# Negative part times slope moved to ScalarE, one VectorE addition a pair of tiles, and three groups of VectorE products and sums moved to GpSimd, in a fused recurrence and feed-forward kernel

## The chip, the cores and the metric

The kernel runs on one core of a Trainium2 chip. The core has TensorE (PE: matrix products, with weight loads that the profile keeps apart as PEld), VectorE (DVE), ScalarE (ACT), GpSimd (POOL) and SyncE (SP, which here only issues transfers). Each engine works through its own list of instructions in order, and semaphores hold an instruction until what it needs is there. The metric is the device time of one execution in microseconds. Before the change the median of three runs is 622.16 us (620.33 to 623.74).

## The reference: what is computed

A gated linear recurrence runs for 4 batches and 8 heads over 768 positions with head size 48, and its output, as 3072 tokens of width 384, goes through a feed-forward block with 2048 hidden units and a leaky activation that has a slope of its own for every hidden unit.

```python
f = 1.0 / (1.0 + np.exp(-f_logit))
for t in range(S):
    state = f[:, :, t, :, None] * state + np.einsum('bhd,bhde->bhde', k[:, :, t], v[:, :, t])
    y[:, :, t] = np.einsum('bhd,bhde->bhe', q[:, :, t], state)
x = y.transpose(0, 2, 1, 3).reshape(B * S, H * D)
h = x @ w_in
g = np.maximum(h, 0.0) + alpha * np.minimum(h, 0.0)
out = g @ w_out
```

## The kernel before

Positions are cut into chunks of 128, and batches into pairs, so there are 6 x 2 = 12 steps (`steps`, L726). A step handles 256 tokens and passes through four stages, written as generators: `prepare` (key letter P: loads, sigmoid, products of decays, scaled copies of q and k), `carry` (S: scores between halves of a chunk, and the state), `attend` (O: scores inside 32 positions, the product with v and the state, the transposed result `xT`) and `network` (n: the feed-forward block). The order in which pieces of these generators are written is a string (`FIRST` and `USUAL`, L31 to L37). For TensorE, VectorE and ScalarE it is the order in their instruction lists (L734); GpSimd and SyncE get their lists from the framework's own scheduler. In the usual order a round holds the network of one step, the scores and state of the next, and the preparation of the one after that.

The parts that the change and the prediction touch, in the order of a usual round:

- `network`, first half. For each of 8 pairs of hidden tiles TensorE makes `ph` (L618), 128 hidden units by two tiles of 256 tokens, in one PSUM bank of a pool of four (`net`). ScalarE writes `neg`, the negative part with its sign turned (L623; `neg` has two buffers). VectorE then computes `neg * om + ph`, once for each tile of the pair (L625), into `gate`; `om` is one minus the slope.
- After the pairs 3 and 7, `sums` (L693) makes four sums or differences of gate tiles, 128 x 512 elements each, into `S` (L702). They feed a product of two-by-two blocks that needs seven block products in place of eight. In step 0 (`plain`) the product with `w_out` is done the ordinary way, without sums.
- `network`, second half (L655 to L689): block products `pa`, `pb`, `pc`, `pd`, `pa`, `pc`, `pe`, each of eight matmuls of 128 x 192, in banks of the same pool, and VectorE's combinations of them (L661). The eighth matmul of `pa` reads the last gate pair; `pc` reads the sums. The first `ph` of the next network takes over the bank of `pb`, so it waits until L661 has read it.
- `prepare`. ScalarE: sigmoid (L279), two copies (L280, L282), four strided copies (L314). VectorE: L287 to L294, two scans (L317, L319), L321, L347, then products L330 to L406, a 32 x 32 transpose (L401), and at the end the products of decays over a half chunk `f64` (L414), 48 x 8 elements each.
- `attend`: VectorE picks scores into `ad` (L526, L541), ScalarE copies them into `A` (L563, eight copies in a step, four for each batch `u` of the pair), TensorE multiplies `A` with v and the state (`py`, L574), ScalarE copies `py` to `y` (L583), and ten transfers on the queues of SP, ACT and POOL lay it out as `xT` for the next network (L603).
- `moved` (L488), called once in `carry` and once in `attend`: the state is multiplied by its decay `f64` (L494, 48 x 768 elements) and the new part is added (L498).
- GpSimd issues the loads of f, q, k and v (L266, L276) and two transfers of `xT` in each step; apart from set-up it computes nothing.

Of the kernel before, what the change touches and what calls it, by code (L numbers as in the profile page):

```python
# [14 lines left out]
AF = mybir.ActivationFunctionType  # L15
ALU = mybir.AluOpType
# [5 lines left out]
U = 2  # L22
# [36 lines left out]
def kernel(  # L59
# [30 lines left out]
    nc = tc.nc  # L90
    B, NC, _, HP, _ = qT.shape
    DM = v.shape[-1]
    H = 2 * HP
    D = DM // H
# [36 lines left out]
    NH, DH = NF // 2, DM // 2  # L131
# [122 lines left out]
    def halves(cc):  # L254

        return slice(CH * cc, CH * cc + CH), slice(CH * (1 - cc), CH * (1 - cc) + D)

    def prepare(bp, c, x):
# [152 lines left out]
        for cc in range(0 if c else 1, NC2 if c < NC - 1 else 1):  # L411
            for par in range(2):
                g64 = by64[rows(par), :, cc, :, NB]
                nc.vector.tensor_tensor(f64[halves(cc)[1], :, par:H:2].rearrange("p u h -> p (u h)"),  # L414
                                        g64[:, :, 0], g64[:, :, 1], ALU.mult)
        yield
        for cc in range(0 if c else 1, NC2):
# [14 lines left out]
    def carry(bp, c, x):  # L432
# [55 lines left out]
        def moved(cc):  # L488

            of, to = halves(cc)[1], halves(1 - cc)[1]  # L490
            was, then = (vs[bp][p, a, :, 0:DM].rearrange("p u (h e) -> p u h e", e=D)
                         for p, a in ((of, cc), (to, 1 - cc)))
            if c or cc:
                nc.vector.tensor_tensor(then, was, f64[of].unsqueeze(3).broadcast_to((D, U, H, D)), ALU.mult)  # L494
            for par in range(2):
                now = pd[rows(par), cc, 0:U * HP * D].rearrange("p (u h e) -> p u h e", u=U, e=D)
                if c or cc:
                    nc.vector.tensor_tensor(then[:, :, par:H:2], then[:, :, par:H:2], now, ALU.add)  # L498
                else:
                    nc.scalar.copy(then[:, :, par:H:2], now)  # L500
# [108 lines left out]
    def network(bp, c, x):  # L609
        i = f"{bp}_{c}"  # L610
        xT = x["T"]
        plain = (bp, c) == steps[0]
        for f in range(NH):
            ph = bank(f"ph{f}_{i}")
            tiles = (2 * f, 2 * f + 1) if plain else (f, f + NH)
            for kt in range(NK):
                for j, m in enumerate(tiles):
                    nc.tensor.matmul(ph[:, j * T:(j + 1) * T], lhsT=w_in_sb[:, kt, m * 128:(m + 1) * 128],  # L618
                                     rhs=xT[:, kt], start=(kt == 0 and j == 0), stop=(kt == NK - 1 and j == 1),
                                     skip_group_check=True)  # L620
            neg = work.tile([128, 2, T], F32, tag="neg", name=f"neg{f}_{i}")
            phv = ph.rearrange("p (j t) -> p j t", j=2)
            nc.scalar.activation(neg, phv, AF.Relu, scale=-1.0)  # L623
            for j, m in enumerate(tiles):
                nc.vector.scalar_tensor_tensor(gate[:, m % NH, m // NH], neg[:, j], om[:, m:m + 1], phv[:, j],  # L625
                                               ALU.mult, ALU.add)
            if not plain and f % 4 == 3:
                sums(slice(f - 3, f + 1))
            yield

        def store(u, o):
            t0 = ((U * bp + u) * NC + c) * C
            nc.sync.dma_start(out=out[t0:t0 + C], in_=o)

        if plain:
            po = [bank(f"po{u}_{i}") for u in range(U)]
            for n, (f, u) in enumerate([(f, u) for f in range(NF) for u in range(U)]):
                nc.tensor.matmul(po[u][:, 0:DM], lhsT=gate[:, f % NH, f // NH, u * C:(u + 1) * C], rhs=w_out_sb[:, f],  # L638
                                 start=(f == 0), stop=(f == NF - 1))
                if n % 8 == 7 and n != U * NF - 1:  # L640
                    yield
            for u in range(U):
                o = work.tile([128, DM], F32, tag="o", name=f"o{u}_{i}")
                nc.scalar.activation(o, po[u][:, 0:DM], AF.Copy, scale=UP)
                store(u, o)
            yield
            return

        a11, a12, a22 = (lambda f, j=j, u=u: gate[:, f, j, u * C:(u + 1) * C] for j, u in ((0, 0), (1, 0), (1, 1)))
        s1, s2, s3, s4 = (lambda f, n=n: late["S"][:, n, f] for n in range(4))  # L650
        b11, t1, b21, b22 = (lambda f, r=r, d=d: w_out_sb[:, NH * r + f, DH * d:DH * (d + 1)]
                             for r, d in ((0, 0), (0, 1), (1, 0), (1, 1)))
        t2, t3, t4 = (lambda f, t=t: late[t][:, f] for t in ("t2", "t3", "t4"))

        def product(to, of, by, more=False):  # L655
            for f in range(NH):
                nc.tensor.matmul(to[:, 0:DH], lhsT=of(f), rhs=by(f), start=(f == 0 and not more), stop=(f == NH - 1),  # L657
                                 skip_group_check=True)

        def plus(to, of, by, scale=UP):  # L660
            nc.vector.scalar_tensor_tensor(to, of[:, 0:DH], scale, by, ALU.mult, ALU.add)  # L661

        o0, o1 = (work.tile([128, DM], F32, tag="o", name=f"o{u}_{i}") for u in range(U))
        kept, u2, u3 = (late["C"][:, n] for n in range(3))
        pa, pb = (bank(f"p{n}_{i}") for n in "ab")
        product(pa, a11, b11)
        product(pb, a22, t4)
        nc.scalar.activation(kept, pa[:, 0:DH], AF.Copy, scale=UP)
        yield
        pc, pd = (bank(f"p{n}_{i}") for n in "cd")  # L670
        product(pc, s2, t2)
        product(pd, s1, t1)
        plus(u2, pc, kept)
        yield
        product(pa, a12, b21, more=True)
        product(pc, s3, t3, more=True)
        plus(o0[:, DH:DM], pd, u2)
        nc.scalar.activation(o0[:, 0:DH], pa[:, 0:DH], AF.Copy, scale=UP)  # L678
        yield
        pe = bank(f"pe_{i}")  # L680
        product(pe, s4, b22)
        plus(u3, pc, kept)
        plus(o1[:, 0:DH], pb, u3, -UP)
        plus(o1[:, DH:DM], pd, u3)
        store(1, o1)
        yield
        plus(o0[:, DH:DM], pe, o0[:, DH:DM])
        store(0, o0)
        yield  # L689
# [3 lines left out]
    def sums(fs_):  # L693

        s = late["S"]
        u0, u1 = slice(0, C), slice(C, T)
        of = lambda j, u: gate[:, fs_, j, u]
        for to, x_, y_, op in ((s[:, 0, fs_], of(0, u1), of(1, u1), ALU.add),
                               (s[:, 1, fs_], s[:, 0, fs_], of(0, u0), ALU.subtract),
                               (s[:, 2, fs_], of(0, u0), of(0, u1), ALU.subtract),  # L700
                               (s[:, 3, fs_], of(1, u0), s[:, 1, fs_], ALU.subtract)):
            nc.vector.tensor_tensor(to, x_, y_, op)  # L702

    def halves_of_w_out():

# [93 lines left out]
```

## Time and profile before

| | |
|---|---|
| median of three runs | 622.16 us (620.33 to 623.74) |
| the profiled execution: span from its first to its last instruction | 622.1 us |
| its time beside the span | no other time is given for this execution; the median of the runs is 0.06 us from its span |
| granted TensorE clock | 1.000 |
| PE busy | 592.1 us (95%) |
| PEld busy | 529.8 us (85%) |
| VectorE busy | 497.1 us (80%), 997 instructions |
| ScalarE busy | 246.6 us (40%), 466 instructions |
| GpSimd busy | 63.0 us (10%), 117 instructions |

The share of busy time is a mean over stages of different kinds. The first 43.7 us hold the first preparation and scores, with TensorE busy 20.8 us; step 0's network runs to 102.6 us; ten rounds of about 47.6 us follow, the last of them without a preparation; and from 579.9 us on there is only the last network. An idle time in brackets behind an instruction is that of its engine just before it, with what ended it. Idle time of an engine that bounds nothing costs nothing.

### The profile page before, as it was taken

Reading aid. Unit: us, or ns where it says so; the run is one execution under the profiler, and the core shown is the slowest. Engines: PE = TensorE matmul, PEld = TensorE weight load, DVE = VectorE, ACT = ScalarE, POOL = GpSimd, SP = SyncE. Lnnn points to the kernel's source line nnn. Section 1 sums busy time; section 2 is a strip of 40 time slices with the busy share of each in tenths; the row PEclk is TensorE's granted clock in tenths of the full one; section 3 lists DMA queues with packets and bytes.
Section 4 is the critical chain, followed back from the end, with each engine's and each line's share of the span. In section 5 each row is a group of like instructions: output and inputs, shape, how many; then the busy total and the mean of one; then the engine's idle time right before and its main releaser. Section 6 shows DMA issues by size and latency. Waiting matters only on the chain.

```text
span 622.1 us, 19062 instructions
## 1 busy us (share of the span) xinstructions
PE 592.1 (95%) x8212; PEld 529.8 (85%) x8212; DVE 497.1 (80%) x997; ACT 246.6 (40%) x466; POOL 63.0 (10%) x117
## 2 busy tenths in 40 slices
PE   3568999999999999999999999999999999999997
PEld 3457866898899899899899899899889889889997
DVE  7588998899898798798798798798888888762261
ACT  5677862441641272262261351352253243223110
POOL 9120010001000011001001001001001000000000
PEclk9999999999999999999999999999999999999999
DMA  9964632014404314214313313413313401201000
GB/s 290 367 234 155 190 85 52 36 36 108 98 8 96 72 35 107 67 35 95 79 35 90 84 35 88 86 36 86 87 36 85 87 3 26 53 2 27 26 0 26
DMA packets 68116, 50.43 MB, mean 81 GB/s; under 512 B 47168, under 2 KB 60608, under 8 KB 68032
## 3 DMA queue, kind: packets, MB, share of 16 engines
q1 hardware_dynamic: 56656, 25.01, 15.6%
q0 software_dynamic: 6864, 22.35, 12.7%
q10 hardware_dynamic: 4512, 1.85, 1.7%
q8 instruction: 65, 1.06, 0.7%
q14 instruction: 19, 0.16, 0.1%
HBM read 36.21 MB, written 4.72 MB: 66 GB/s over the span
## 4 chain that ended last, share of the span: by engine, by line
PE 88%; DVE 6%; ACT 3%; issue 2%; DMA 1%; ACTq 0%; DVEq 0%
PE ph L618 39%; PE pc L657 9%; PE pa L657 8%; PE pd L657 5%; PE pe L657 4%; PE pb L657 4%; PE py L574 4%; PE po L638 3%; PE raw L520 3%; PE qu L535 3%; PE pd L484 3%; PE off L444 1%; PE xt L592 1%; DVE gate L625 1%; DMA f<-in_fT 1%
## 5 line engine op out<-in xcount | busy, mean ns | idle before, releaser
L618 PE MATMUL ph<-xT,w_in_sb 128*128 128x256 f32 x1152 | 258.7, 382 | 0.7 <-DVE Csum L661 0.7
L618 PEld LDWEIGHTS ph<-xT,w_in_sb 128*128 128x128 f32 x1152 | 216.4, 190 | 33.4 <-issue 2.3
L623 ACT ACTIVATE neg<-ph 128x512 f32<-128x512 f32 x96 | 57.4, 598 | 200.8 <-PE ph L618 139.5
L625 DVE SCALAR_TENSOR_TENSOR gate<-neg,om,ph 128x256 f32<-128x256 f32 x192 | 82.7, 478 | 50.6 <-ACT neg L623 50.4
L657 PE MATMUL pc<-t,S 128*128 128x192 f32 x352 | 61.7, 329 | 0.0
L657 PE MATMUL pa<-w_out_sb,gate 128*128 128x192 f32 x352 | 61.3, 327 | 0.1
L657 PEld LDWEIGHTS pa<-w_out_sb,gate 128*128 128x128 f32 x352 | 57.9, 190 | 1.0 <-DVE gate L625 0.4
L657 PEld LDWEIGHTS pc<-t,S 128*128 128x128 f32 x352 | 57.3, 190 | 0.6
L526 DVE COPY_PREDICATED ad<-mraw,raw 128x256 f32<-128x256 int32 (+1 forms) x96 | 42.4, 442 | 11.1 <-PE raw L520 8.6
L541 DVE COPY_PREDICATED ad<-mquad,qu 128x224 f32<-128x224 int32 (+6 forms) x140 | 42.0, 300 | 6.2
L419 ACT COPY A<-q 48x512 f32<-48x512 f32 x44 | 27.2, 619 | 36.1 <-DVE q L368 35.7
L563 ACT COPY A<-ad 32x256 f32<-32x256 f32 x96 | 38.7, 403 | 1.4
L330 DVE TENSOR_TENSOR us<-us,fs 128x768 f32<-128x768 f32 (+5 forms) x60 | 36.8, 614 | 0.0
L678 ACT ACTIVATE o<-pa 128x192 f32<-128x192 f32 x11 | 3.7, 332 | 75.2 <-PE pa L657 72.3
L661 DVE SCALAR_TENSOR_TENSOR Csum<-pc,Csum 128x192 f32<-128x192 f32 x22 | 7.9, 357 | 30.3 <-PE pc L657 30.1
L287 DVE TENSOR_TENSOR qd<-qd,f 128x768 f32<-128x768 f32 (+2 forms) x36 | 27.2, 756 | 6.0 <-ACT qd L282 6.0
L520 PEld LDWEIGHTS raw<-qd,k 48*32 48x32 f32 x1536 | 18.5, 109 | 15.3 <-issue 13.1
L520 PE MATMUL raw<-qd,k 48*32 48x80 f32 x1536 | 24.0, 243 | 7.6 <-issue 4.4
L702 DVE TENSOR_TENSOR S<-gate 128x512 f32<-128x512 f32 x44 | 30.3, 688 | 0.8
L657 PE MATMUL pe<-w_out_sb,S 128*128 128x192 f32 x176 | 30.4, 326 | 0.0
L657 PE MATMUL pd<-w_out_sb,S 128*128 128x192 f32 x176 | 30.4, 326 | 0.0
L657 PE MATMUL pb<-t,gate 128*128 128x192 f32 x176 | 30.4, 326 | 0.0
(101 smaller groups left out, 758.3 us busy)
## 6 DMA issues: line engine op xcount, KB each, us to landing
w_out_raw<-in_w_out SPq DMA_DIRECT2D x8, 767.8 KB, 5.8
w_in_raw<-in_w_in SPq DMA_DIRECT2D x8, 767.2 KB, 11.9
q<-in_qT POOLq DMA_DIRECT2D x11, 512.0 KB, 4.2
f<-in_fT POOLq DMA_DIRECT2D x11, 512.0 KB, 4.5
k<-in_kT POOLq DMA_DIRECT2D x11, 512.0 KB, 4.9
out<-o SPq DMA_DIRECT2D x24, 192.0 KB, 2.7
vs<-in_v POOLq DMA_DIRECT2D x22, 192.0 KB, 4.6
ksn<-kt SPq DMA_DIRECT2D x80, 32.0 KB, 2.0
```

The lines of the kernel that those rows point to most:

```text
L287: nc.vector.tensor_tensor(qdv[d], qdv[d - 1][:, :, :, 1:5 - d], f[:, :, 1:5 - d].rearrange("p (g i) r -> p g i r", i=NB), ALU.mult)
L330: nc.vector.tensor_tensor(us[:, :, UO[m]:UO[m] + 4 * n].rearrange("p g (i r) -> p g i r", r=4), us[:, :, skip:skip + 4 * n].rearrange("p g ...
L419: nc.scalar.copy(A[halves(cc)[1], :, par * HP:(par + 1) * HP, CH * cc:CH * (cc + 1)], q3[rows(par)].rearrange("p (u h c) s t -> p u h c (s ...
L520: nc.tensor.matmul(raw[DB * j:DB * (j + 1), par, hp * C:hp * C + QW], lhsT=k[r_, g * DB:(g + 1) * DB], rhs=qd[r_, g], start=True, stop=True)
L526: nc.vector.copy_predicated(adu[:, :, :, d:4], mraw[:, d, :, d:4].bitcast(I32).unsqueeze(1).broadcast_to((128, H, NB, n)), rv[:, :, QO[d]: ...
L541: nc.vector.copy_predicated(ad[:, u, :, :, 4 * m:DB], mquad[:, lo:lo + n].bitcast(I32).unsqueeze(1).unsqueeze(1).broadcast_to((128, 2, HP, ...
L563: nc.scalar.copy(A[s_, u, :, s_], ad[s_, u].rearrange("p r h t -> p (r h) t"))
L618: nc.tensor.matmul(ph[:, j * T:(j + 1) * T], lhsT=w_in_sb[:, kt, m * 128:(m + 1) * 128], rhs=xT[:, kt], start=(kt == 0 and j == 0), stop=( ...
L623: nc.scalar.activation(neg, phv, AF.Relu, scale=-1.0)
L625: nc.vector.scalar_tensor_tensor(gate[:, m % NH, m // NH], neg[:, j], om[:, m:m + 1], phv[:, j], ALU.mult, ALU.add)
L657: nc.tensor.matmul(to[:, 0:DH], lhsT=of(f), rhs=by(f), start=(f == 0 and not more), stop=(f == NH - 1), skip_group_check=True)
L702: nc.vector.tensor_tensor(to, x_, y_, op)
```

## The change

Four edits:

1. The product of the negative part and `om` is done by ScalarE, in place in `neg`, one instruction for each tile of a pair (192 in all). VectorE's `neg * om + ph` becomes a plain addition of `neg` and `ph`: for step 0 still one for each tile, for the other eleven steps one over both tiles of a pair, 128 x 512 elements.
2. The four sums of `sums` go from VectorE to GpSimd (88 instructions).
3. The product of state and decay in `moved` goes from VectorE to GpSimd (20 instructions).
4. The products of decays `f64` go from VectorE to GpSimd (40 instructions).

The lists of instructions change accordingly. On ScalarE the two multiplications stand right behind the `neg` that they work on, ahead of what followed it. On GpSimd the four second sums of a round are split: three, then the four decay products of the next step, then the fourth sum, then the state product for the next step, the load of f, the state product of this step, and only then the load of v and the two transfers of `xT`. On TensorE the order of the matmuls is unchanged.

```diff
@@ prepare
-                nc.vector.tensor_tensor(f64[halves(cc)[1], :, par:H:2].rearrange("p u h -> p (u h)"),
+                nc.gpsimd.tensor_tensor(f64[halves(cc)[1], :, par:H:2].rearrange("p u h -> p (u h)"),
                                         g64[:, :, 0], g64[:, :, 1], ALU.mult)
@@ carry, moved(cc)
             if c or cc:
-                nc.vector.tensor_tensor(then, was, f64[of].unsqueeze(3).broadcast_to((D, U, H, D)), ALU.mult)
+                nc.gpsimd.tensor_tensor(then, was, f64[of].unsqueeze(3).broadcast_to((D, U, H, D)), ALU.mult)
@@ network
             nc.scalar.activation(neg, phv, AF.Relu, scale=-1.0)
             for j, m in enumerate(tiles):
-                nc.vector.scalar_tensor_tensor(gate[:, m % NH, m // NH], neg[:, j], om[:, m:m + 1], phv[:, j],
-                                               ALU.mult, ALU.add)
+                nc.scalar.activation(neg[:, j], neg[:, j], AF.Copy, scale=om[:, m:m + 1])
+            if plain:
+                for j, m in enumerate(tiles):
+                    nc.vector.tensor_tensor(gate[:, m % NH, m // NH], neg[:, j], phv[:, j], ALU.add)
+            else:
+                nc.vector.tensor_tensor(gate[:, f], neg, phv, ALU.add)
             if not plain and f % 4 == 3:
                 sums(slice(f - 3, f + 1))
@@ sums
-            nc.vector.tensor_tensor(to, x_, y_, op)
+            nc.gpsimd.tensor_tensor(to, x_, y_, op)
```

## The prediction, made blind

> **What bounds the kernel now.** First the page: busy shares and the chain that ended last.
>
> ```profile
> span 622.1 us, 19062 instructions
> PE 592.1 (95%) x8212; PEld 529.8 (85%) x8212; DVE 497.1 (80%) x997; ACT 246.6 (40%) x466; POOL 63.0 (10%) x117
> ...
> PE 88%; DVE 6%; ACT 3%; issue 2%; DMA 1%; ACTq 0%; DVEq 0%
> ```
>
> TensorE carries 88% of the chain. VectorE's 80% is a mean, so the stages come next (stretch, its length, then busy time of PE, PEld, DVE, ACT, POOL).
>
> ```profile
> 102.60:152.00 49.40, 48.89 (x785) 43.80 (x783) 44.32 (x87) 18.47 (x36) 4.47 (x7) 1.00 0.24 63
> 389.00:436.60 47.60, 47.53 (x664) 43.26 (x669) 41.42 (x86) 17.87 (x36) 4.47 (x7) 1.00 0.29 68
> ```
>
> A usual round leaves TensorE idle for 0.07 us of 47.6. Less work on VectorE can win nothing in such a round; what is late in it costs its full lateness. So I looked in the timeline of that round for places without slack.
>
> ```profile
> 389.89 0.36 DVE L661 SCALAR_TENSOR_TENSOR o<-pb,Csum 128x192 f32<-128x192 f32 x1
> ...
> 390.60 5.05 PEld L618 LDWEIGHTS ph<-xT,w_in_sb 128*128 128x128 f32 x24 [0.17 <-DVE o L661]
> ...
> 416.18 0.60 ACT L623 ACTIVATE neg<-ph 128x512 f32<-128x512 f32 x1 [2.04 <-PE ph L618]
> 416.68 2.17 ACT L314 COPY us<-qd 128x256 f32<-128x256 f32 x4
> 416.81 0.87 DVE L625 SCALAR_TENSOR_TENSOR gate<-neg,om,ph 128x256 f32<-128x256 f32 x2 [0.33 <-ACT neg L623]
> ...
> 418.96 3.33 ACT L563 COPY A<-ad 32x256 f32<-32x256 f32 x8
> 421.23 2.16 PE L574 MATMUL py<-A,vs 128*64 128x64 f32 x64
> ...
> 426.29 0.36 DVE L661 SCALAR_TENSOR_TENSOR Csum<-pc,Csum 128x192 f32<-128x192 f32 x1 [1.51 <-PE pc L657]
> ```
>
> There are two. ScalarE runs from the last `neg` (416.18) to the last `A` copy (422.29) without a pause, and the second half of `py` wants that copy at 421.23 + 1.04 = 422.27: slack nil. VectorE's list ends at 390.25, and the next `ph` waited 0.17 us for it: slack nil again.
>
> Last, how GpSimd's reads of SBUF stand beside VectorE's two-input instructions, which only the start shows.
>
> ```profile
> 6.49 1.00 POOL L166 COPY mquad<-inq 128x28 f32<-128x28 f32 x7
> 7.44 3.24 POOL L174 COPY mhalf<-inq 128x12 f32<-128x12 f32 x6
> 7.49 0.96 DVE L287 TENSOR_TENSOR qd<-qd,f 128x768 f32<-128x768 f32 x1 [1.01 <-ACT qd L282]
> ...
> 11.91 1.19 DVE L321 TENSOR_TENSOR us<-us,f 128x1024 f32<-128x1024 f32 x1
> 12.16 2.19 POOL L190 COPY dense<-ident 128x48 f32<-128x48 f32 x2
> 13.03 1.24 DVE L347 TENSOR_TENSOR k<-k,kr 128x1024 f32<-128x1024 f32 x1
> ```
>
> Seven small copies take 1.00 us while VectorE is idle; six smaller ones take 3.24 us beside its products, and the last two 2.19 us, ending at 14.35 where L347 ends (14.27). Each copy waits for a VectorE instruction to end: the two exclude each other. These copies are too short to show whether a long GpSimd read holds VectorE in turn.
>
> **The sum** is made against the execution's span of 622.1 us; the median of the runs, 622.16, is the same within 0.01%, so nothing is added for what lies around the span.
>
> *Negative part times slope on ScalarE.* 192 instructions of 128 x 256 out of SBUF, scaled from a column. Nearest rows: L563's copy of 256 elements at 403 ns (constant scale), L623's at 598 ns for 512. I take 0.42 us each, 0.85 us a pair; ends 0.70 (overlapping as L314's do) and 1.0. On paper 192 x 0.42 = 81 us, in 375 us of idle ScalarE; in most rounds it lies in the 2 us gaps ahead of `neg`. It does not in the run from the last `neg`. There: `neg` of pair 4, then L279 to L282, move 0.85 us; VectorE's L287, which waits for L282, and the pair-5 addition behind it end at 416.4 in place of 415.7; the last `neg` needs that buffer, so it starts at 416.4 (+0.2); its two multiplications add 0.85; L314, L668 and L563 follow, about 1.1 us late (0.9 to 1.2), and with no slack at `py` so is TensorE. Inside this lies the last gate pair: ready at 418.6 (was 417.25 for its first tile), where the eighth matmul of `pa` wants its weights at 418.1; 0.5 us of the 1.1. Against it stands the 0.17 us wait of `ph`. Seven rounds (199 to 532 us) have this order: 7 x (1.1 - 0.17) = **+6.5 us**.
>
> *The addition.* 128 x 512 with one input in PSUM: L498 takes 552 ns at 384 elements, L702 688 at 512; I take 0.69 (0.65 to 0.75) for two L625 starts of 0.43. That saves 0.17 us a pair, off the path except as counted above.
>
> *What leaves VectorE.* Behind the last gate pair of a usual round: four sums 2.54 us (417.72 to 420.26), one L494 0.99, four L414 0.72, and the 1.51 us in which it waits for `pc`. From 417.68 to 437.85 (390.25 a round later) it now needs 20.17 us; 14.4 remain. They begin at 418.6.
>
> *What GpSimd must do meanwhile.* Four second sums, four L414, two L494; VectorE's L498 waits for the second L494. No GpSimd addition is in this trace. Lower end: a one-input copy (178 ns at 4 elements, 198 at 28: 0.83 ns an element), 0.60 us at 512. Upper end: the select of 128 elements at 742 ns scaled by four, 2.97 us, although that one itself sat beside L317. The copy is the nearest kind; with two inputs I count its elements twice: 0.17 + 512 x 1.66 = 1.02 us for a sum, 1.45 for L494, 0.18 for L414. Together 4.1 + 2.9 + 0.7 = 7.7 us. Since neither runs beside the other's reads, they add up: 418.6 + 14.4 + 7.7 = 440.7, where `ph` could go at 438.0 + 1.1 = 439.15. Stall 1.55 us, 7 x 1.55 = **+10.9**. At 0.60 us a sum (0.81 for L494, 4.7 us in all) there is none; at 2.97 (4.45 for L494) 21.5 us and a stall of 15.3 us a round.
>
> The Trainium skill, SBUF — State Buffer, section "Who interferes with whom", states that a VectorE instruction with two SBUF inputs contends with a GpSimd instruction that reads SBUF, whole instruction against whole instruction, the later one fully blocked. The trace agrees for GpSimd as the later one (3.24 us for six tiny copies); VectorE as the later one no run here shows. By that rule this term stands; without it the term is nothing.
>
> *The other rounds.* Round 1 (102.6 to 152.3): the first sums now fall among L721 and L287, the last gate pair is ready at about 132.75 (was 131.78); VectorE's 20.9 us to its last L661 (152.68) lose 5.2; 132.75 + 15.7 + 7.7 = 156.15: **+3.5**. Round 2: gates at 179.5, 14.35 us left, 201.55 against 200.1 for the next `ph`: 1.45, and 0.3 at `pa`: **+1.75**. The last two networks have no preparation behind them: 0.4 and 0.3 at `pa` and `py`: **+0.7**. Step 0 and the start: ScalarE's `y` copies (87.0) slip by some 5 us, covered up to 102.6; GpSimd's two L414 hold the second step's loads (14.4) about 1 us, covered since f is wanted at 33.06. Cost nil.
>
> *Queues passed.* On POOL the load of v and two `xT` transfers stand behind the second L494: issued at about 433 where it was 424.8, landing 4 us later at 437, wanted at 439. That cover is thin: it is what is late next, if GpSimd is slower than I take it. SP's sixteen `ksn` transfers need L401, which moves with VectorE and TensorE alike. Loads of f, k and q have over 20 us. The sums reach `pc` in time: third one ready at about 424.1, wanted at 425.6.
>
> Sum: 622.1 + 6.5 + 10.9 + 3.5 + 1.75 + 0.7 = **645**.
>
> **Rivals.** *One: GpSimd and VectorE run side by side.* Then VectorE ends at 433 at the latest plus its wait for `pc`, about 437.4, and stalls nobody; round 1 wins back its waits of 0.74 and 1.0 us. 622.1 + 6.5 - 1.7 + 0.3 + 0.7 = 628. For it: no VectorE row in the start is longer than its mean (L287 959 ns there and over all). Against it: the six copies.
>
> *Two: a GpSimd addition costs twice VectorE's rows*, 1.38 and 1.9 us: 10.0 us a round, stall 3.85. 7 x (0.93 + 3.85) + 5.8 + 4.05 + 0.7 = 44, so 666. For it: two inputs plus overheads that small copies hide; against it: memsets on both engines run alike (0.88 ns an element). The Trainium skill, GPSIMD Engine Reference, section 3.1, has 4497 against 2293 ns for 2048 elements, a ratio of 1.96; as an estimate by that page the sum is about 664. No run here shows it.
>
> *Three, the other side: not slower.* ScalarE's lateness doesn't reach `py`, and VectorE's relief takes away the waits of `ph` (8 x 0.17) and of round 1 (1.7): 619. Place: the last `A` copy against the second half of `py`. It decides when the two multiplications cost below 0.1 us in sum, as if they ran inside `neg`'s tail. For it: ScalarE idles 2.04 us just ahead of that `neg`. Against it: the idle lies before, not behind. That the edits don't reach the engines can be left out: the lists of instructions show them moved.
>
> **How the numbers follow.** 0.5% (3.1 us, near the spread of the runs) is about what can be told from no change. Chances: forecast 0.43 (sums between 0.6 and 1.25 us: 630 to 660), rival one 0.24, rival two 0.22, rival three 0.06, dearer still 0.05. Eight in ten: from 626, the lower side of rival one, to 668, just above rival two. Faster takes half of rival three, 0.03; the same the other half and the low end of rival one, 0.08; slower 0.89.
>
> **What would show it.** Right: VectorE idle or long products where GpSimd's sums run; `ph` waiting for L661 by 1 to 4 us in rounds 3 to 9; second half of `py` waiting for L563; TensorE idle 20 us more in all; VectorE about 60 us less busy unless blocked time counts as busy. Wrong: GpSimd sums near 0.7 us with VectorE rows unchanged (rival one), sums of 1.4 us (two), `py` not waiting (three), or `ph` waiting for the `xT` transfers from POOL.

## The result, and the profile after

The changed kernel takes 640.16 us (median of four runs, 638.81 to 642.40) where the kernel before, run beside it, takes 621.86 (620.33 to 623.74). The ratio is 1.0298, with a 95% interval of 1.0265 to 1.0330: 18.3 us slower. The prediction said 645, slower, with a range of 626 to 668.

The profiled execution of the changed kernel took 638.81 us, of which its span is 637.0, so 1.8 us lie around the span. Against the span before (622.1) that is 14.9 us more, less than the 18.3 between the medians, for two reasons: this execution is the lowest of its four, and the 622.1 us is one of the longer executions of the kernel before, whose spans in the runs timed here go from 618.3 to 623.1 with a median of 619.7. The places below are compared by the spans.

First the page of the changed kernel: span, busy shares, and shares of the chain that ended last.

```profile
span 637.0 us, 19255 instructions
...
PE 596.5 (94%) x8212; PEld 528.4 (83%) x8212; DVE 457.1 (72%) x761; ACT 329.1 (52%) x658; POOL 256.1 (40%) x265
...
PE 49%; DVE 23%; ACT 18%; issue 6%; SPq 1%; DMA 1%; ACTq 0%; DVEq 0%
```

VectorE is 40 us less busy, ScalarE 82 more and GpSimd 193 more. The chain, 88% TensorE before, now runs through VectorE and ScalarE for 41% of its length.

A usual round in windows, from the first `ph` of one network to that of the next (stretch, length, then busy time of PE, PEld, DVE, ACT, POOL):

```profile
401.38:450.60 49.22, 48.06 (x656) 43.28 (x656) 38.37 (x64) 24.72 (x52) 22.20 (x21) 1.00 0.27 66
```

The same stretch took 47.71 us before, with 0.07 us of it idle on TensorE; now TensorE is idle for 1.16. The view of waits says where over the whole run (engine, line, what it waited for: us, times, longest):

```profile
PE pa L661 <- DVE gate L630: 4.7, 9, 1.2
...
PE py L574 <- ACT A L563: 2.4, 8, 0.3
PE ph L618 <- DVE Csum L665: 2.4, 6, 0.4
...
PE po L642 <- DVE w_out_sb L234: 1.6, 1, 1.6
```

And the timeline of that round (start, length, engine, line; in brackets the idle time before it and what ended it):

```profile
427.23 0.60 ACT L623 ACTIVATE neg<-ph 128x512 f32<-128x512 f32 x1 [1.06 <-DVE gate L630]
427.86 0.91 ACT L625 ACTIVATE neg<-neg,om 128x256 f32<-128x256 f32 x2
428.68 2.15 ACT L314 COPY us<-qd 128x256 f32<-128x256 f32 x4
...
429.54 0.59 PE L661 MATMUL pa<-w_out_sb,gate 128*128 128x192 f32 x2 [0.36 <-DVE gate L630]
429.58 3.33 POOL L706 TENSOR_TENSOR S<-gate 128x512 f32<-128x512 f32 x2 [5.24 <-DVE gate L630]
...
430.07 1.77 DVE L319 TENSOR_TENSOR_SCAN ss<-fs,ones 128x289 f32<-128x289 f32 x1
...
431.77 2.22 DVE L321 TENSOR_TENSOR us<-us,f 128x1024 f32<-128x1024 f32 x1
...
432.87 2.26 POOL L706 TENSOR_TENSOR S<-S,gate 128x512 f32<-128x512 f32 x1
433.91 2.29 DVE L347 TENSOR_TENSOR k<-k,kr 128x1024 f32<-128x1024 f32 x1
...
434.27 1.03 PE L574 MATMUL py<-A,vs 128*64 128x64 f32 x28 [0.33 <-ACT A L563]
...
450.20 0.35 DVE L665 SCALAR_TENSOR_TENSOR Csum<-pc,Csum 128x192 f32<-128x192 f32 x1
...
450.58 0.36 DVE L665 SCALAR_TENSOR_TENSOR o<-pb,Csum 128x192 f32<-128x192 f32 x1
...
450.60 5.45 PE L618 MATMUL ph<-xT,w_in_sb 128*128 128x256 f32 x24 [0.40 <-DVE Csum L665]
```

The two multiplications stand between the last `neg` and L314, so the last gate pair and the last `A` copy are late for TensorE (0.36 and 0.33 us of idle). Behind the gate pair GpSimd and VectorE take turns: L319, L321 and L347, whose own lengths before were 0.74, 1.20 and 1.22 us, each last 1.02 to 1.07 us longer, while a GpSimd sum that takes 1.25 us on idle ground takes up to 2.26. At the end `ph` waits 0.40 us for VectorE. The three waits make 1.09 of the 1.51 us; the other 0.42 shows as busy time (48.06 against 47.64), in the matmuls beside the waits: from the first `pa` to the first `pb` it is 3.22 us where it was 2.60, and from the first `py` to the first `pc` 2.56 where it was 2.08. These 0.62 and 0.48, with the 0.40 at `ph`, are the whole loss of the round.

### The profile page after: what moved, and what is told of

Read it like the earlier page. It is cut to its first block, busy times and chain, and to the rows that moved or that the text cites. A ratio compares the mean times of both kernels' runs of the same rounds, so it can differ in the third digit from the quotient of the medians.

```text
span 637.0 us, 19255 instructions
## 1 busy us (share of the span) xinstructions
PE 596.5 (94%) x8212; PEld 528.4 (83%) x8212; DVE 457.1 (72%) x761; ACT 329.1 (52%) x658; POOL 256.1 (40%) x265
## 4 chain that ended last, share of the span: by engine, by line
PE 49%; DVE 23%; ACT 18%; issue 6%; SPq 1%; DMA 1%; ACTq 0%; DVEq 0%
PE ph L618 26%; PE pc L661 6%; DVE us L330 6%; ACT A L563 4%; ACT us L314 3%; ACT neg L625 3%; DVE qd L287 3%; ACT neg L623 2%; PE raw L520 2%; PE pd L484 2%; PE pe L661 2%; PE pa L661 2%; PE qu L535 2%; ACT qd L282 2%; PE pd L661 2%
## 5 line engine op out<-in xcount | busy, mean ns | idle before, releaser
L706 POOL TENSOR_TENSOR S<-gate 128x512 f32<-128x512 f32 x44 | 63.3, 1457 | 171.4 <-DVE gate L630 171.4
L630 DVE TENSOR_TENSOR gate<-neg,ph 128x512 f32<-128x512 f32 x88 | 59.6, 686 | 93.4 <-ACT neg L625 93.3
L625 ACT ACTIVATE neg<-neg,om 128x256 f32<-128x256 f32 x192 | 87.1, 500 | 3.2
L661 PE MATMUL pa<-w_out_sb,gate 128*128 128x192 f32 x352 | 64.5, 330 | 5.0 <-DVE gate L630 4.7
L266 POOL DMA_DIRECT2D k<-in_kT x11 | 8.0, 730 | 145.0 <-PE raw L520 145.0
L661 PEld LDWEIGHTS pa<-w_out_sb,gate 128*128 128x128 f32 x352 | 57.6, 190 | 9.4 <-DVE gate L630 8.8
L661 PE MATMUL pc<-t,S 128*128 128x192 f32 x352 | 62.1, 329 | 0.6 <-DVE Csum L665 0.3
L661 PEld LDWEIGHTS pc<-t,S 128*128 128x128 f32 x352 | 57.2, 190 | 1.8 <-DVE Csum L665 0.6
L330 DVE TENSOR_TENSOR us<-us,fs 128x768 f32<-128x768 f32 (+5 forms) x60 | 55.7, 928 | 0.0
L563 ACT COPY A<-ad 32x256 f32<-32x256 f32 x96 | 38.4, 400 | 1.4
L494 POOL TENSOR_TENSOR vs<-vs,f 48x768 f32<-48x768 f32 x20 | 37.6, 1882 | 1.3
L706 POOL TENSOR_TENSOR S<-S,gate 128x512 f32<-128x512 f32 x22 | 36.6, 1665 | 0.0
L414 POOL TENSOR_TENSOR f<-ps 48x8 f32<-48x8 f32 x40 | 27.3, 684 | 21.0 <-DVE ps L317 18.6
L574 PEld LDWEIGHTS py<-A,vs 128*64 128x64 f32 x768 | 25.7, 145 | 7.3 <-ACT A L563 5.1
```

Source lines behind the costliest of these rows:

```text
L330: nc.vector.tensor_tensor(us[:, :, UO[m]:UO[m] + 4 * n].rearrange("p g (i r) -> p g i r", r=4), us[:, :, skip:skip + 4 * n].rearrange("p g ...
L494: nc.gpsimd.tensor_tensor(then, was, f64[of].unsqueeze(3).broadcast_to((D, U, H, D)), ALU.mult)
L563: nc.scalar.copy(A[s_, u, :, s_], ad[s_, u].rearrange("p r h t -> p (r h) t"))
L625: nc.scalar.activation(neg[:, j], neg[:, j], AF.Copy, scale=om[:, m:m + 1])
L630: nc.vector.tensor_tensor(gate[:, f], neg, phv, ALU.add)
L706: nc.gpsimd.tensor_tensor(to, x_, y_, op)
```

## The experiments

Ten kernels were run, each timed beside the kernel before (medians of 621.41 to 622.21 us). Each table row gives the ratio to it, and then, from the profiled execution, the start of round 2, and the lengths of round 2, of rounds 3 to 9 (mean of seven) and of what follows (from the first `ph` of round 10 to the end). They are worked out from the starts of `ph` in the chain of work.

| kernel | time, us | ratio (95% interval) | start of round 2 | round 2 | rounds 3 to 9 | rest |
|---|---|---|---|---|---|---|
| before | 621.86 | 1 | 152.3 | 47.6 | 47.69 | 88.3 |
| changed | 640.16 | 1.0298 (1.0265 to 1.0330) | 156.6 | 48.2 | 49.05 | 88.9 |
| GpSimd's three edits | 629.98 | 1.0136 (1.0106 to 1.0166) | 152.8 | 49.1 | 48.28 | 88.4 |
| the gate's edit | 632.50 | 1.0180 (1.0142 to 1.0218) | 153.7 | 47.9 | 48.82 | 88.8 |
| only the decay products | 620.52 | 0.9984 (0.9966 to 1.0003) | 151.9 | 47.5 | 47.67 | 88.2 |
| memsets for the sums | 631.78 | 1.0169 (1.0139 to 1.0198) | 151.8 | 47.5 | 48.64 | 88.8 |
| only the sums | 627.23 | 1.0087 (1.0068 to 1.0106) | 156.0 | 47.4 | 47.59 | 88.7 |
| changed, last pair old | 636.51 | 1.0229 (1.0202 to 1.0255) | 154.9 | 49.1 | 48.49 | 88.1 |
| last pair and step 0 old | 632.92 | 1.0181 (1.0156 to 1.0206) | 153.3 | 49.0 | 48.45 | 88.0 |
| light: gate's edit with both old, decay products | 621.77 | 1.0006 (0.9990 to 1.0021) | 149.5 | 47.5 | 47.84 | 88.2 |
| changed, state product on VectorE | 635.96 | 1.0227 (1.0199 to 1.0254) | 156.5 | 48.2 | 48.65 | 88.8 |
| changed, state product twice | 686.72 | 1.1023 (1.0989 to 1.1056) | 166.2 | 53.9 | 53.71 | 88.8 |

One execution of each kernel is profiled. Two of the kernels take the same time as the kernel before: their rounds 3 to 9 agree with its within 0.15 us, but their round 2 starts 0.4 and 2.8 us earlier. So the start of round 2 is the least sure of these columns.

### The two halves of the change, each alone

GpSimd's three edits without the gate's:

```diff
-                nc.vector.tensor_tensor(f64[halves(cc)[1], :, par:H:2].rearrange("p u h -> p (u h)"),
+                nc.gpsimd.tensor_tensor(f64[halves(cc)[1], :, par:H:2].rearrange("p u h -> p (u h)"),
...
-                nc.vector.tensor_tensor(then, was, f64[of].unsqueeze(3).broadcast_to((D, U, H, D)), ALU.mult)
+                nc.gpsimd.tensor_tensor(then, was, f64[of].unsqueeze(3).broadcast_to((D, U, H, D)), ALU.mult)
...
-            nc.vector.tensor_tensor(to, x_, y_, op)
+            nc.gpsimd.tensor_tensor(to, x_, y_, op)
```

> The three groups of work go to GpSimd as in the change, but the gate stays as before (one scalar_tensor_tensor of VectorE for each tile, no multiplication on ScalarE). Theory A (two separate costs: ScalarE's multiplications make the second half of py late by 1.1 us a round, and GpSimd's reads hold up VectorE, so that ph waits for the last L661): the py lateness is gone, py starts 7.4 us after pa as before, VectorE rows L319, L321, L347 stay as long as in the change (1.5, 1.9, 2.0 us), ph waits for L661 by some 0.5 to 0.8 us a round, and the time is 5 to 7 us above before, about 628. Rival B (ScalarE's instructions are hidden and GpSimd's side is the whole loss): the time stays at about 640. Rival C (exclusion on GpSimd's side costs nothing that matters): about 622.

The gate's edit without GpSimd's:

```diff
-                nc.vector.scalar_tensor_tensor(gate[:, m % NH, m // NH], neg[:, j], om[:, m:m + 1], phv[:, j],
-                                               ALU.mult, ALU.add)
+                nc.scalar.activation(neg[:, j], neg[:, j], AF.Copy, scale=om[:, m:m + 1])
+            if plain:
+                for j, m in enumerate(tiles):
+                    nc.vector.tensor_tensor(gate[:, m % NH, m // NH], neg[:, j], phv[:, j], ALU.add)
+            else:
+                nc.vector.tensor_tensor(gate[:, f], neg, phv, ALU.add)
```

> Only the gate is changed: the multiplications on ScalarE and one VectorE addition a pair; sums, state decay and decay products stay on VectorE. Theory A: py starts 8.5 us after pa in rounds 3 to 9 (7.4 before), step 0 ends about 2 us later since ScalarE's weight pieces come late, VectorE rows are as before; 7 x 1.1 + 2 + 0.6 for the last two networks: about 631. Rival B: within 1 us of before. Rival C (the whole loss is on ScalarE's side): about 640.

Measured: 1.36% and 1.80%. Both halves cost, and their sum, 3.16%, is within the intervals of the 2.98% of the whole. The gate's edit alone makes a usual round 1.13 us longer, and VectorE's rows (L319, L321, L347) keep their old lengths, so this cost has nothing to do with GpSimd. Step 0, which the expectation had end 2 us later, ends 0.3 us later, and `po` does not wait.

GpSimd's half costs 0.59 us in the mean of rounds 3 to 9, but neither as the prediction nor as Theory A had it: `ph` never waits for L661 in these rounds, and L321 and L347 take 1.24 and 1.32 us in the mean, not 1.9 and 2.0. That the time is near A's 628 is luck. Its waits on TensorE:

```profile
PE pc L657 <- POOL S L702: 5.5, 7, 1.5
```

and the rows in which this comes about, from its timeline:

```profile
424.68 1.76 DVE L319 TENSOR_TENSOR_SCAN ss<-fs,ones 128x289 f32<-128x289 f32 x1
425.90 3.77 POOL L414 TENSOR_TENSOR f<-ps 48x8 f32<-48x8 f32 x4
426.36 1.20 DVE L321 TENSOR_TENSOR us<-us,f 128x1024 f32<-128x1024 f32 x1
...
427.48 1.24 DVE L347 TENSOR_TENSOR k<-k,kr 128x1024 f32<-128x1024 f32 x1
428.64 0.96 DVE L330 TENSOR_TENSOR us<-us,fs 128x768 f32<-128x768 f32 x1
...
429.75 1.26 POOL L702 TENSOR_TENSOR S<-S,gate 128x512 f32<-128x512 f32 x1
...
431.06 1.57 PE L657 MATMUL pc<-t,S 128*128 128x192 f32 x8 [0.71 <-POOL S L702]
```

Here four tiny decay products stand ahead of the third sum in GpSimd's list. They come while VectorE runs, each of the four ends within 0.1 us of the end of a VectorE instruction, and the last ends at 429.67, just behind L330 (429.60): three VectorE products pass at their full speed and GpSimd waits for all of them. The third sum is then late for `pc`. In the whole change ScalarE's lateness moves `pc` back by 1.1 us, and the wait of `pc` for a sum shrinks to 0.2 us in all: there the two halves cover each other.

### The decay products alone

```diff
-                nc.vector.tensor_tensor(f64[halves(cc)[1], :, par:H:2].rearrange("p u h -> p (u h)"),
+                nc.gpsimd.tensor_tensor(f64[halves(cc)[1], :, par:H:2].rearrange("p u h -> p (u h)"),
```

> Only the small decay products (L414, 40 instructions of 48 x 8) go to GpSimd; everything else as before. Theory A: VectorE's list ends 0.7 us earlier in each round, which removes the 0.17 us wait of ph and part of the waits of round 1, GpSimd's four short reads hold VectorE by less than that, and the first stage ends up to 0.8 us earlier as it did in the changed kernel: 1 to 3 us below before, 619 to 621. If even short GpSimd reads cost VectorE a whole handover (0.5 us each), 2 us a round are lost: 625 or more.

The interval includes no change. By themselves the 40 small products are harmless; what hurt in the run above was their place ahead of the third sum.

### Sums that read nothing

In the changed kernel each sum is replaced by two memsets of its target, so that GpSimd writes as much and reads nothing; the sums are left out and the output is not the reference's.

```diff
-            nc.gpsimd.tensor_tensor(to, x_, y_, op)
+            for _ in range(2):
+                nc.gpsimd.memset(to, 0.0)
```

> As the changed kernel, but each of the four sums is replaced by two GpSimd memsets of the same 128 x 512 tile, about as long as a sum alone (1.1 us) but with nothing read from SBUF; the sums themselves are left out, so the output is not the reference's. Theory A with exclusion of reads: VectorE's L319, L321 and L347 fall back to 0.75, 1.20 and 1.22 us although GpSimd is as busy at the same moment, only the products beside L494 stay long, ph no longer waits for L661, and the time falls by 0.6 us a round and some 2 us in round 1, to about 632 to 634. Rival (any GpSimd work on SBUF, reads or not, slows VectorE, or the products are long for another reason): the rows stay at 1.5 to 2.0 us and the time stays at about 640.

Groups by form of the kernel before (mean ns of one before the last bar):

```profile
L347 DVE TENSOR_TENSOR k<-k,kr 128x1024 f32<-128x1024 f32 x12 | 14.6, 1221 | 0.0
L321 DVE TENSOR_TENSOR us<-us,f 128x1024 f32<-128x1024 f32 x12 | 14.4, 1198 | 0.0
...
L319 DVE TENSOR_TENSOR_SCAN ss<-fs,ones 128x289 f32<-128x289 f32 x12 | 8.8, 736 | 0.0
```

of the changed kernel:

```profile
L347 DVE TENSOR_TENSOR k<-k,kr 128x1024 f32<-128x1024 f32 x12 | 24.3, 2029 | 0.0
L321 DVE TENSOR_TENSOR us<-us,f 128x1024 f32<-128x1024 f32 x12 | 22.8, 1900 | 1.1 <-ACT us L314 1.1
...
L319 DVE TENSOR_TENSOR_SCAN ss<-fs,ones 128x289 f32<-128x289 f32 x12 | 18.2, 1514 | 0.0
```

and of this one:

```profile
L347 DVE TENSOR_TENSOR k<-k,kr 128x1024 f32<-128x1024 f32 x12 | 17.3, 1444 | 0.0
L321 DVE TENSOR_TENSOR us<-us,f 128x1024 f32<-128x1024 f32 x12 | 15.0, 1254 | 3.3 <-ACT us L314 2.9
...
L319 DVE TENSOR_TENSOR_SCAN ss<-fs,ones 128x289 f32<-128x289 f32 x12 | 8.8, 736 | 0.0
```

These rows alone would not show that writing is harmless, since the memsets, which have no inputs to wait for, mostly run elsewhere in the round. Where they do run beside products of two inputs in SBUF, from its timeline:

```profile
432.73 0.69 DVE L330 TENSOR_TENSOR us<-us,fs 128x512 f32<-128x512 f32 x1
...
432.93 3.34 POOL L707 MEMSET S<- 128x512 f32 x7
433.33 0.68 DVE L368 TENSOR_TENSOR q<-us,ps 128x512 f32<-128x512 f32 x1
433.93 0.55 DVE L330 TENSOR_TENSOR us<-us,fs 128x384 f32<-128x384 f32 x1
```

Seven memsets run without a pause and the products keep their lengths (0.69 and 0.56 us before for the L330 forms). In the whole run, 81 VectorE products with both inputs in SBUF lie beside a memset for more than 0.1 us and beside no GpSimd read, and none differs by more than 0.014 us from the median of its form before. So it is GpSimd's reading that holds VectorE. The Trainium skill, SBUF — State Buffer, section "Who interferes with whom", states the same: a VectorE instruction with two SBUF inputs contends with a GpSimd instruction that reads SBUF, not with one that only writes it. The 1444 ns of L347 come from two of its twelve rows, both beside a state product of GpSimd. A usual round is still 0.95 us longer than before, and `ph` does not wait for L665: what is left is near the 1.13 us of the gate's edit alone. From the changed kernel to this one the span falls by 8.4 us, 4.8 of it ahead of round 2 and 0.4 in each of rounds 3 to 9.

### The sums alone

```diff
-            nc.vector.tensor_tensor(to, x_, y_, op)
+            nc.gpsimd.tensor_tensor(to, x_, y_, op)
```

> Only the four sums go to GpSimd; the gate, the state product and the decay products stay as before. Theory A (GpSimd and VectorE exclude each other while both read SBUF, and a GpSimd sum keeps VectorE out for about 1.05 us): four sums take 4.2 us of VectorE's time where they took 2.54 on it, and its wait for pc (1.51 us) covers nearly all of the difference, so a usual round stays within 0.3 us of before; round 1 loses some 1 us; 622 to 625 us, VectorE's wait for pc nearly gone. Theory B (the sums on GpSimd are too late for pc by themselves, as in the run with GpSimd's three edits): pc waits about 0.7 us a round for the third sum, 627 to 630 us. Both: VectorE's rows behind the last gate pair stretched by about 1.05 us for each sum.

Measured 627.23 us, in the range of Theory B, but the place is not B's: usual rounds are as long as before (47.59), as A has it, and the loss lies in round 1, which is 6.4 us longer than before and holds one wait of 4.46 us. Its timeline:

```profile
132.69 0.75 DVE L317 TENSOR_TENSOR_SCAN ps<-fs,ones 128x289 f32<-128x289 f32 x1
132.77 5.56 POOL L702 TENSOR_TENSOR S<-S,gate 128x512 f32<-128x512 f32 x1
133.36 0.73 DVE L319 TENSOR_TENSOR_SCAN ss<-fs,ones 128x289 f32<-128x289 f32 x1
134.01 1.20 DVE L321 TENSOR_TENSOR us<-us,f 128x1024 f32<-128x1024 f32 x1
135.13 1.21 DVE L347 TENSOR_TENSOR k<-k,kr 128x1024 f32<-128x1024 f32 x1
136.26 0.95 DVE L330 TENSOR_TENSOR us<-us,fs 128x768 f32<-128x768 f32 x1
...
138.39 2.28 PE L657 MATMUL pc<-t,S 128*128 128x192 f32 x8 [4.46 <-POOL S L702]
```

The third sum comes 0.08 us behind L317 and is then passed by four VectorE instructions that start after it; it ends 1.12 us after the last of them. In the usual round of the same kernel GpSimd and VectorE alternate. The exclusion is thus not one-for-one, and the rule in the prediction, by which the later one is blocked, does not hold here: the sum that waited was passed by instructions that came after it, and the measurement decides. What decides between the two patterns was not found.

### The last pair, and step 0, in the old form

In the changed kernel, the last pair of each network after step 0 keeps VectorE's two instructions.

```diff
-            for j, m in enumerate(tiles):
-                nc.scalar.activation(neg[:, j], neg[:, j], AF.Copy, scale=om[:, m:m + 1])
+            if not plain and f == NH - 1:
+                for j, m in enumerate(tiles):
+                    nc.vector.scalar_tensor_tensor(gate[:, m % NH, m // NH], neg[:, j], om[:, m:m + 1], phv[:, j],
+                                                   ALU.mult, ALU.add)
+            else:
+                for j, m in enumerate(tiles):
+                    nc.scalar.activation(neg[:, j], neg[:, j], AF.Copy, scale=om[:, m:m + 1])
...
```

> The changed kernel, but the last pair of each network after step 0 keeps VectorE's two instructions, so ScalarE has no multiplication behind the last neg. Theory A (ScalarE's cost lies only in its unbroken run from the last neg to the last A copy): about 1 us less in each of rounds 3 to 9 and 0.3 to 1 elsewhere, but with pa and py earlier the sums on GpSimd become late for pc, as in the run with GpSimd's three edits: 631 to 635 us. If the sums are still in time: 628 to 631. Rival (the cost is spread over all pairs, since every neg is later): 638 to 641 us, and py still waits for L563.

Measured 636.51 us, span 631.5. The waits of `py` for L563 and of `ph` for L665 are gone. In their place:

```profile
PE pc L666 <- POOL S L711: 5.9, 7, 1.5
...
PE po L647 <- DVE w_out_sb L234: 2.1, 1, 2.1
```

`pc` waits 0.78 us a round again, in five of the seven rounds; a usual round loses 0.80 us in place of 1.36. ScalarE's cost does lie in that one unbroken run, and taking it away uncovers the sums' lateness. The time is just above the 631 to 635 that were expected.

Then step 0 in the old form as well (`if plain or f == NH - 1:`):

> As the run with the old last pair, and step 0 with the old gate as well. Theory A (step 0's 2.1 us are due to ScalarE's multiplications that push back its pieces of w_out): the wait of po for L234 (1.6 us) goes, and the time is 1.5 to 2.5 us below that run. Rival (step 0's lateness is due to GpSimd's reads on VectorE alone): po waits as before and the time is within 0.7 us of that run.

Measured 632.92 us, 3.6 us below that run by the medians and 2.0 by the spans, where 1.5 to 2.5 were expected. The wait of `po` for L234 is gone and round 2 starts 1.6 us earlier. ScalarE's multiplications push the pieces of `w_out` (L224, L225) back, and VectorE gets them late. But they are only half of it: with the gate's edit alone, and in the run below with the state product on VectorE, ScalarE multiplies in step 0 too and `po` does not wait. In the changed kernel two state products of GpSimd come beside VectorE at 89.56 and 92.51, and an L234 takes 2.31 us where the others take 1.04 and an L330 2.10 where it took 0.82, 2.55 us together. Counted from the first `ph` of step 0, the L234 that `po` needs starts after 46.75 us with the gate's edit alone and after 49.29 in the changed kernel. So the wait needs both ScalarE's lateness and the state product; with the state product done twice (below) it is 4.8 us.

### Only where ScalarE has slack

Sums and state product stay on VectorE, decay products on GpSimd, and ScalarE multiplies in all pairs but the last and all of step 0.

```diff
-            for j, m in enumerate(tiles):
-                nc.vector.scalar_tensor_tensor(gate[:, m % NH, m // NH], neg[:, j], om[:, m:m + 1], phv[:, j],
-                                               ALU.mult, ALU.add)
+            if plain or f == NH - 1:
+                for j, m in enumerate(tiles):
+                    nc.vector.scalar_tensor_tensor(gate[:, m % NH, m // NH], neg[:, j], om[:, m:m + 1], phv[:, j],
+                                                   ALU.mult, ALU.add)
+            else:
+                for j, m in enumerate(tiles):
+                    nc.scalar.activation(neg[:, j], neg[:, j], AF.Copy, scale=om[:, m:m + 1])
+                nc.vector.tensor_tensor(gate[:, f], neg, phv, ALU.add)
```

> The gate with ScalarE's multiplication in all pairs but the last of each network and all of step 0; sums and state product on VectorE as before; only the decay products on GpSimd. Theory A (ScalarE's multiplications cost nothing where its slack is, ahead of a neg, and VectorE's relief is worth at most the 0.17 us of ph's wait a round and part of round 1): 618 to 622.5 us, ratio 0.995 to 1.001. Rival (each ScalarE multiplication delays the neg chain whatever its place): 626 us and more.

No change (0.9990 to 1.0021): 154 multiplications on ScalarE cost nothing there and win nothing. It also shows a misreading. From its timeline, the end of a round:

```profile
386.24 0.35 DVE L666 SCALAR_TENSOR_TENSOR Csum<-pc,Csum 128x192 f32<-128x192 f32 x1
...
386.62 0.36 DVE L666 SCALAR_TENSOR_TENSOR o<-pb,Csum 128x192 f32<-128x192 f32 x1
...
388.28 5.45 PE L618 MATMUL ph<-xT,w_in_sb 128*128 128x256 f32 x24
```

VectorE is through with `pb` at 386.98 and `ph` starts at 388.28, yet 0.17 us of idle stand ahead of its weight load here too, put down to issue. The 0.17 us that the prediction read as `ph` waiting for VectorE is not a wait for VectorE.

### The state product: back on VectorE, and twice on GpSimd

The changed kernel with L494 on VectorE:

```diff
-                nc.gpsimd.tensor_tensor(then, was, f64[of].unsqueeze(3).broadcast_to((D, U, H, D)), ALU.mult)
+                nc.vector.tensor_tensor(then, was, f64[of].unsqueeze(3).broadcast_to((D, U, H, D)), ALU.mult)
```

> The changed kernel with the state product (L494) back on VectorE; gate, sums and decay products as changed. Theory A (ph's wait of 0.4 us in a usual round is the end of VectorE's list, made of its own work and of the time in which GpSimd keeps it out): the two products keep VectorE out for 1.28 us each and would take 0.98 us each on it, so its list ends 0.6 us earlier, the wait of ph goes and a usual round is 1.0 to 1.2 us longer than before, not 1.5: 635 to 638 us. Rival (the stall comes from the sums alone, or ph waits for something else): 639 to 642 us, ph waits as in the changed kernel.

Measured 635.96 us; `ph` waits for VectorE no more and a usual round is 0.96 us longer than before, just under the 1.0 to 1.2 expected. So the wait of `ph` comes from the end of VectorE's list, as Theory A has it. Its account of 0.6 us (1.28 us kept out each, against 0.98 of VectorE's own) is too small: from the end of the first L374 to the end of the last L665 on `pc` it is 9.36 us in the round that starts at 399.26, where it was 10.95 in the changed kernel's round shown above, because only one of VectorE's own two products (0.95 us) stands there and the other ahead of the last gate pair (2 x 1.28 - 0.95 = 1.61). This run too has the long wait of `pc` in round 1 (4.49 us) that the run with the sums alone shows; its step 0 ends 4.0 us earlier than that of the changed kernel, and round 2 starts at the same time.

The changed kernel with the state product done twice on GpSimd, with the same result:

```diff
-                nc.gpsimd.tensor_tensor(then, was, f64[of].unsqueeze(3).broadcast_to((D, U, H, D)), ALU.mult)
+                for _ in range(2):
+                    nc.gpsimd.tensor_tensor(then, was, f64[of].unsqueeze(3).broadcast_to((D, U, H, D)), ALU.mult)
```

> The changed kernel with each state product on GpSimd done twice, with the same result. Theory A (each one keeps VectorE out for 1.28 us and nothing covers it): a usual round is 2.5 us longer, L330 of 640 and 512 elements or their neighbours stretched once more, ph waits for L665 by 2.9 us; nine rounds, 658 to 665 us. Rival (GpSimd is the one that waits and VectorE goes on): 640 to 650 us, the L494 rows on GpSimd long, and the load of v and the xT transfers behind them late (ph waits for xT).

Measured 686.72 us, ratio 1.1023 (1.0989 to 1.1056), beyond both. Of the 47.9 us by which its span is longer than that of the changed kernel, 9.1 lie ahead of round 1 and 32.6 in rounds 3 to 9. Rounds 4 to 8 are 54.2 to 54.6 us long, 5.4 more than the same rounds of the changed kernel, twice what A said. The wait itself is A's size, now at `qu`, which needs L330's last piece, just ahead of `ph`:

```profile
488.99 1.75 PE L536 MATMUL qu<-us,k 48*32 48x112 f32 x64 [2.78 <-DVE us L330]
...
490.67 7.71 PE L619 MATMUL ph<-xT,w_in_sb 128*128 128x256 f32 x24
```

The rest is in the matmuls behind it: the 24 of `ph` take 7.71 us in place of 5.45, and `qu` 1.75 in place of 1.08, together 2.9. The windows of that kernel give the granted clock (the figure behind POOL's):

```profile
443.80:490.60 46.80, 43.28 (x633) 39.22 (x632) 36.26 (x49) 21.17 (x45) 25.12 (x23) 0.98 0.21 60
490.60:498.40 7.80, 7.80 (x40) 6.19 (x40) 5.17 (x15) 3.54 (x7) 0.00 (x0) 0.70 0.33 61
```

After an idle time of 2.8 us, TensorE runs at a mean clock of 0.70 for 7.8 us; in the changed kernel, whose waits there are 0.4 us, the clock is 1.00. Finer windows show it at 1.00 up to 488.0, at 0.50 from 488.5 to 495.0, and at 1.00 again from 495.5. The run with the sums alone shows 0.50 too behind its wait of 4.46 us (139.4 to 141.0). The Trainium skill, TensorE: Matmul & The Clock Gate, Part 1, says that the clock follows how busy the array has been in windows of about 3.4 us, with half rate after an idle one. The half rate agrees (0.50); but the idle time here, 2.8 us, is shorter than such a window, and the clock fell after some 2.3 us of it, so the rows do not bear out that a whole window has to be idle.

## Why the prediction was right or wrong

*Direction and size.* Slower, and in the range, for the two reasons given. By the medians the change is 18.3 us, where 23 were predicted; the sum by places, in us of the two spans, is 14.9. The prediction took the median of the runs and the span before for the same and added nothing; 1.8 us lie around the spans here, so the execution of 622.1 us was one of about 623.9.

| term | predicted | measured |
|---|---|---|
| step 0 and start | nil | +1.3 |
| round 1 | +3.5 | +2.9 |
| round 2 | +1.75 | +0.6 |
| rounds 3 to 9, ScalarE | +6.5 | +7.9 with the gate's edit alone |
| rounds 3 to 9, exclusion | +10.9 | +1.6, what is left of +9.5 for all of rounds 3 to 9 |
| last two networks | +0.7 | +0.6 |
| sum | +23 | +14.9 |

The +1.6 is a remainder, since the two halves cover each other in part: GpSimd's edits alone cost 7 x 0.59 = 4.1 us in these rounds.

*Negative part on ScalarE: right.* Two multiplications take 0.91 us a pair (0.85 estimated), from `pa` to `pb` it is 0.62 us longer (0.5 predicted), and from a round's first `ph` to the first copy of `y` (L583) it is 33.97 us where it was 32.83: +1.14, against 1.1. The credit of 0.17 us a round against it does not exist, as the light version shows; without it the term is 7 x 1.1 = 7.7, and the gate's edit alone gives 7.9.

*The exclusion: the mechanism right, its term mis-sized.* The step that failed is "418.6 + 14.4 + 7.7 = 440.7, where `ph` could go at 439.15". Its parts in the round shown: GpSimd held VectorE for 6.1 us (rows longer than before by 1.04, 1.02, 1.07, 0.44, 1.28 and 1.27), and in the 1.11 us in which VectorE waits for `pc` GpSimd ran the last two small products and began the fourth sum, 7.2 in all against 7.7. A sum's price of 1.02 us was near what it keeps VectorE out (1.05), though it lasts 1.25. Wrong too was the other end: "VectorE's list ends at 390.25, and the next `ph` waited 0.17 us for it: slack nil again". In the changed kernel `ph` starts at 450.60 while L665 on `pb` is running (450.58 to 450.94), and 0.05 us after the one on `pc` has ended (450.20 + 0.35); the other rounds that wait look alike. So by these rows it waits for `pc`'s reader and not, as the description of the kernel above has it too, for `pb`'s. The profile before shows the same at the end of round 1, the one place where its `ph` waits:

```profile
152.32 0.36 DVE L661 SCALAR_TENSOR_TENSOR o<-pb,Csum 128x192 f32<-128x192 f32 x1
152.34 8.04 PE L618 MATMUL ph<-xT,w_in_sb 128*128 128x256 f32 x36 [0.74 <-DVE Csum L661]
```

In the round before that the prediction showed, `pc`'s reader ended one step ahead of `pb`'s, which started at 389.89, and `ph` started at 390.60: 0.7 us of slack. The 1.15 us between the predicted stall (1.55) and the measured one (0.40) come apart when the two rounds are laid on each other by their first `ph` (390.60 and 401.38, so 10.78 us are taken off the times after). L665 on `pb` ends at 440.16, not 440.7, which is 0.54; `ph` starts 0.34 before that end; and it was itself ready only at 439.42, not 439.15, which is 0.27. So the stall is 0.40 us in five rounds and not 1.55 in seven (the 2.4 us in the view of waits also hold round 1). The other two are rounds 8 and 9, where GpSimd has only two decay products and, in round 9, only one state product; the prediction counted them as full ones. The first of these is about the 7.2 us against 7.7, the second the wrong reader. A stall that is the small difference of two sums of 20 us is upset by a few tenths in either of them.

*Round 1 and round 2.* The same account, with the same slack too little. *Step 0 and the start: wrong.* "ScalarE's `y` copies slip by some 5 us, covered up to 102.6" was about the wrong instruction: the pieces of `w_out` behind L314 are what `po` needs, made late by ScalarE and by the two state products on GpSimd together, and it waited 1.6 us.

*Queues passed.* The two `xT` transfers on POOL came in time; `ph` never waited for them in the changed kernel. "The sums reach `pc` in time" holds for the changed kernel (0.2 us of waiting), and only because `pc` is itself late.

*Rivals.* One (side by side) falls with VectorE's rows. Two (GpSimd at twice VectorE's rows) was half right on the price, 1.25 us against 0.69, a ratio of 1.8, but what counts is the 1.05 us. Three (`py` not reached) falls with the wait of `py` for L563. TensorE was to be idle for 20 us more; it is 10.5 (637.0 - 596.5 against 622.1 - 592.1). The page's busy time does count blocked time, as the prediction left open: VectorE shows 40 us less, not 60.

## What to carry to other kernels

Where one engine is the bound, moving work off another wins nothing, and the price is set at the places without slack: the work that stands between the last producer and the first consumer of the bounding engine (here behind the last `neg`). Moving two-input work from VectorE to GpSimd kept VectorE out for most of the instruction (1.05 of the 1.25 us of a sum), and a small GpSimd instruction ahead of an urgent one could wait for a whole run of VectorE's. Before calling a wait "slack nil", find which instruction it needs; here it was one earlier than the one named beside it, and the same 0.17 us stand there with VectorE long done.

## What the runs showed that was not expected

- A GpSimd instruction can lose several turns in a row: four VectorE instructions that started after it passed it, and a sum of 1.25 us took 5.56.
- A TensorE idle time of 2.8 us costs twice: another 2.9 us in the matmuls behind it, at a mean granted clock of 0.70.
- A wait that neither half makes alone: in step 0 `po` waits only where ScalarE multiplies and GpSimd has the state product (1.6 us, and 4.8 with the product done twice).
- Two losses that cover each other: with ScalarE's lateness alone a usual round is 1.13 us longer, with GpSimd's edits alone 0.59, with both 1.36.
- No version that was run is faster than the kernel before by more than the measurement can tell; the two that equal it, 0.9984 and 1.0006, take 40 small products, or these and the multiplications of 77 pairs, off VectorE and win nothing.
